# One load in place of two at the start of a decode block, and the two result stores in another written order

## The chip, the cores and the metric

The kernel runs on one core of a Trainium2 chip. The metric is the device time of one execution in microseconds (us); before the change it is 213.88 us, the median of three runs (213.80, 213.88 and 213.93 us).

## What is computed

The reference is one decode step of a transformer block for four sequences (B = 4, one token each, width D = 448), all in float32:

```python
h  = x + attention(layernorm(x))            # 16 query heads, 8 key/value heads of 256
h2 = h + mlp(layernorm(layernorm(h)))       # 448 -> 1792 -> gelu -> 448, with biases
# attention: q = x @ wq; scores over the last W = 1024 cached positions, softmax, values, @ wo
# mlp:       gelu(y @ w1 + b1) @ w2 + b2
```

Keys, values and weights are used once each, so nearly every byte that the kernel moves is read from HBM exactly once: 88.2 MB in all.

## The kernel before, in words

The work is tiled by the eight key/value heads, called groups g = 0 to 7. For one group the kernel projects the normed x to queries (`project_q`, line 204), multiplies them with the keys (`scores`, line 224), takes the softmax, transposes the probabilities (`transpose_p`, line 250), multiplies with the values (`values`, line 262), and adds the group's part of the output projection (`heads`, `project_o`). After the last group come the residual, two layer norms folded into one row of steps, the MLP with `w1` and `w2`, and the stores.

The host packs keys, values, query weights and output weights into eleven arrays, `stream0` to `stream10`, in the order in which they are wanted (the table `LOADS`, line 41: each row is one array and lists its parts). Each array is 128 rows, one for each SBUF partition, of 39,936 to 57,344 bytes, and is loaded by one DMA into one slot of a ring of three SBUF slots (`ring`, line 75). The function `part` (line 92) is asked for a piece; where it isn't there yet, it takes the next array, a slot, and issues the load:

```python
            if src is streams_first:
                nc.sync.dma_start(t[:, : WC + X0], first)
            at = WC + X0 if src is streams_first else 0
            nc.sync.dma_start(t[:, at : at + src.shape[-1]], src)
```

So the first slot is filled by two DMAs: `first` (the query weights of group 0, x transposed, b1 and b2; 7,312 bytes a row) and `stream0` (keys of group 0 and query weights of group 1; 39,936 bytes a row). The loads of `stream1` and `stream2` follow at once, since the ring has three slots. Every later load waits on SyncE's queue (SP) until the slot's last readers are done: `stream3` takes the slot of `first` and `stream0`, and its last reader on TensorE is the projection of group 1's queries (line 207); `stream4` takes the slot of `stream1`, whose last reader is the first half of group 0's values (line 269). After the streams, the same ring takes the values of group 7, the last output weights, `w1` and `w2` (lines 126 to 131 and 373 to 389).

What uses `first`: lines 315 to 326 take x out of it, form mean and variance with small matmuls (lines 186 and 187), a power on GpSimd (line 201), write the normed x to `yT` (lines 323 to 325) and project group 0's queries. Lines 329 to 347 spread the biases and x over partitions by four transposes on TensorE (lines 341 to 346). Constants that need no load (`sel`, `fold`, `foldn`, `back`, lines 142 to 172) are made on VectorE (DVE).

TensorE's order is the order in which the code is written (`manual_schedule` for PE); the order on the other engines is set by a scheduler from the written code. A DMA signals its end on one of eight completion semaphores, taken in turn; a DMA that gets a semaphore waits for the DMA that had it before.

The end: the result, in `res`, is stored by two DMAs of 8 rows each, one issued from ScalarE's queue (ACT), one from SP (lines 518 to 520).

Of the kernel before, what the change touches and what calls it, by code (L numbers as in the profile page):

```python
# [30 lines left out]
WC = 4 * D  # L31
QU = KV // 4
X0 = 2 * ND * B + 4
# [3 lines left out]
def parts(kind, g, quarters=range(4)):  # L37
    return [(kind, g, i) for i in quarters]


LOADS = [
    [("q", 0, 0), *parts("k", 0), ("q", 1, 0)],
    [*parts("k", 1), ("q", 2, 0), *parts("v", 0, (0, 1))],
    [*parts("v", 0, (2, 3)), ("o", 0, 0), *parts("k", 2)],
    [("q", 3, 0), *parts("v", 1), ("o", 1, 0), *parts("k", 3, (0,))],
    [*parts("k", 3, (1, 2, 3)), ("q", 4, 0), *parts("v", 2, (0, 1, 2))],
    [*parts("v", 2, (3,)), ("o", 2, 0), *parts("k", 4), ("q", 5, 0)],
    [*parts("v", 3), ("o", 3, 0), *parts("k", 5, (0, 1))],
    [*parts("k", 5, (2, 3)), ("q", 6, 0), *parts("v", 4)],
# [6 lines left out]
def width(part):  # L56
    kind, g, _ = part
    if kind in "kv":
        return QU
    return WC + (X0 if (kind, g) == ("q", 0) else 0)  # L60
# [8 lines left out]
SCALE = DH ** -0.5  # L69

@with_exitstack
def block_kernel(ctx: ExitStack, tc, first, streams, v7, wo67, w1, w2, w2_low, out):
    nc = tc.nc
    const = ctx.enter_context(tc.tile_pool(name="const", bufs=1))
    ring = ctx.enter_context(tc.tile_pool(name="ring", bufs=3))
# [10 lines left out]
    def slot(name):  # L86
        return ring.tile([P, SLOT], F32, tag="t", name=name)

    held = {}
    streams_first = streams[0]  # L90

    def part(kind, g, i=0):
        while (kind, g, i) not in held:
            src = streams.pop(0)
            t = slot("stream")
            wanted = LOADS[len(LOADS) - len(streams) - 1]
            if src is streams_first:
                nc.sync.dma_start(t[:, : WC + X0], first)  # L98
            at = WC + X0 if src is streams_first else 0
            nc.sync.dma_start(t[:, at : at + src.shape[-1]], src)  # L100
            at = 0
            for one in wanted:
                held[one] = t[:, at : at + width(one)]
                at += width(one)
        return held[kind, g, i]
# [10 lines left out]
    def load_k(g, h, c):  # L116
        return part("k", g, 2 * h + c).rearrange("p (b k) -> p b k", b=B)
# [5 lines left out]
    def load_v(g, c):  # L123
        return part("v", g, c).rearrange("p (c b d) -> p c b d", c=2, b=B)
# [176 lines left out]
    def project_o(g, wt):  # L301
        for i in range(4):
# [6 lines left out]
            for j in range(4):  # L309
# [3 lines left out]
                )  # L313

    t0 = part("q", 0)
    xT = t0[:, WC : WC + ND * B].rearrange("p (a b) -> p a b", a=ND)
    d = work.tile([P, ND, B], F32, tag="d", name="d_x")
# [42 lines left out]
    for g in range(HKV):  # L360
# [11 lines left out]
        else:  # L372
# [9 lines left out]
            at = 0  # L382
# [101 lines left out]
    for i in range(2):  # L484
        for j in range(4):
            if i <= j:
                at = PAD + C * j - P * (j - 1 + i) if j else PAD
# [27 lines left out]
                w = tw2[:, W2L + (c - 9) * C : W2L + (c - 8) * C]  # L515
                nc.tensor.matmul(py[3 * Q :], gT_low[:, c - 9, :], w, start=False, stop=False)  # L516
    nc.vector.tensor_copy(res[:, :C], py)  # L517
    for i, queue in ((1, nc.scalar), (0, nc.sync)):
        at = i * H + LIFT
        queue.dma_start(out[2 * B * i : 2 * B * (i + 1)], res[at : at + 2 * B])  # L520

# [68 lines left out]
```

## Time and profile before

| what | before |
|---|---|
| median of three runs | 213.88 us |
| the profiled execution, its own time | 213.79 us |
| its span in the trace, first to last instruction | 212.0 us |
| PE busy / DVE / ACT | 142.4 / 37.0 / 24.5 us |
| moved by DMA | 88.39 MB, mean 417 GB/s |
| SP's DMA queue (q1), share of the 16 DMA engines | 97.0% |
| chain that ended last | DMA 79%, PE 18% |

The span is 1.79 us shorter than the execution's own time; what lies outside is not in the trace. PE is the matmuls of TensorE, DVE VectorE, ACT ScalarE, POOL GpSimd, SP SyncE, which here only issues DMAs. "DMA share" is the mean share of the core's 16 DMA engines that is busy, and GB/s what they move. An idle engine costs nothing unless the end waits for it: what matters is which engine is never idle.

### The profile page before, as it was taken

To read this page: it belongs to the slowest core of one execution; us is meant where nothing else is said; L and a number is where in the kernel's file an instruction comes from. 1 tells how busy PE (TensorE), PEld (TensorE's weight loads), DVE (VectorE), ACT (ScalarE), POOL (GpSimd) and SP (SyncE) were. 2 spreads that over 40 slices of the span, in tenths; PEclk is the share of its full clock that TensorE was granted. 3 is DMA by queue.
4 is the path that set the end of the run, shared out by engine and by line. 5 is a ranking of instruction groups with operands and counts; after the bars stand their busy time and mean duration, and the time that the engine had idled before them with its cause. 6 is when DMAs were issued, how large, how long until landed. Compare 5 with 4: busy or idle time off the path is not lost.

```text
span 212.0 us, 2559 instructions
## 1 busy us (share of the span) xinstructions
PE 142.4 (67%) x1103; PEld 55.5 (26%) x1103; DVE 37.0 (17%) x153; ACT 24.5 (12%) x58; POOL 6.5 (3%) x22
## 2 busy tenths in 40 slices
PE   0469805861860885870794780586499998989994
PEld 0333301220110511220122120131124333335443
DVE  1521400320130110320123011031032032101330
ACT  2011300110001100210003000030002002100310
POOL 6200000000000000000000000000000000000110
PEclk9999975896697579996589698599589999999999
DMA  7999798999989999898999989899999899999991
GB/s 297 437 407 510 340 512 383 460 446 398 480 355 507 393 449 452 386 483 347 510 414 436 468 383 469 365 490 398 464 414 444 378 467 399 408 434 417 416 404 58
DMA packets 3146, 88.39 MB, mean 417 GB/s; under 512 B 368, under 2 KB 576, under 8 KB 960
## 3 DMA queue, kind: packets, MB, share of 16 engines
q1 hardware_dynamic: 3120, 88.24, 97.0%
q8 instruction: 8, 0.13, 0.2%
q14 instruction: 2, 0.02, 0.0%
q10 hardware_dynamic: 16, 0.00, 0.0%
HBM read 88.23 MB, written 0.01 MB: 416 GB/s over the span
## 4 chain that ended last, share of the span: by engine, by line
DMA 79%; PE 18%; ACT 1%; issue 0%; SPq 0%; DVE 0%; ACTq 0%
DMA stream<-stream 69%; DMA w<-w 10%; PE s L230 6%; PE po L269 6%; PE ppt L255 2%; PE py L510 2%; PE pq L207 1%; PE pqt L215 1%; ACT qs L209 1%; PE acc L304 0%; SPq L98 0%; SPq L100 0%; DVE res L517 0%; PE py L516 0%; ACTq L209 0%
## 5 line engine op out<-in xcount | busy, mean ns | idle before, releaser
L230 PE MATMUL s<-stream,qT 128*32 128x512 f32 x256 | 37.4, 730 | 17.1 <-DMA stream<-stream 17.1
L269 PE MATMUL po<-stream,pT 128*32 128x512 f32 x224 | 31.6, 702 | 17.5 <-DMA stream<-stream 17.5
L234 DVE TENSOR_REDUCE mx<-s 128x1 f32<-128x512 f32 x16 | 11.1, 691 | 57.3 <-PE s L230 57.3
L230 PEld LDWEIGHTS s<-stream,qT 128*32 128x32 f32 x256 | 9.7, 132 | 42.6 <-issue 30.6
L207 PE MATMUL pq<-stream,yT 128*32 128x512 f32 (+1 forms) x80 | 10.2, 603 | 9.7 <-DMA stream<-stream 6.6
L269 PEld LDWEIGHTS po<-stream,pT 128*32 128x32 f32 x224 | 6.9, 124 | 35.3 <-DMA stream<-stream 20.4
L286 DVE TENSOR_SCALAR o<-po,rec 128x256 f32<-128x256 f32 x8 | 3.9, 483 | 60.1 <-PE po L269 60.1
L209 ACT COPY qs<-pq 128x512 f32<-128x512 f32 x8 | 4.7, 585 | 83.3 <-PE pq L207 83.3
L287 ACT ACTIVATE o<-po,rec 128x256 f32<-128x256 f32 x8 | 3.8, 473 | 74.4 <-DVE o L286 74.4
L241 ACT ACTIVATE p<-s,nm 128x512 f32<-128x512 f32 x16 | 10.9, 689 | 10.1 <-DVE nm L237 10.1
L255 PE MATMUL ppt<-ident,p 128*128 128x128 f32 x64 | 11.1, 303 | 0.4
L304 PE MATMUL acc<-stream,oT 128*32 128x448 f32 x48 | 7.3, 683 | 5.2 <-DMA stream<-stream 4.0
L215 PE MATMUL pqt<-ident,qs 128*128 128x128 f32 x32 | 6.1, 322 | 5.7 <-ACT qs L209 5.7
L294 PE MATMUL pot<-ident,o 128*128 128x128 f32 x32 | 7.1, 317 | 3.8 <-DVE o L286 3.1
L354 PEld LDWEIGHTS <-idle 128*32 128x32 bf16 x70 | 6.3, 96 | 9.0 <-issue 3.6
L207 PEld LDWEIGHTS pq<-stream,yT 128*32 128x32 f32 x80 | 4.1, 124 | 17.1 <-issue 16.0
L255 PEld LDWEIGHTS ppt<-ident,p 128*128 128x128 f32 x64 | 7.6, 151 | 3.7 <-ACT p L241 3.7
L354 PE MATMUL tail<-idle 128*32 128x512 bf16 x28 | 7.6, 381 | 0.0
L294 PEld LDWEIGHTS pot<-ident,o 128*128 128x128 f32 x32 | 3.4, 148 | 13.3 <-DVE o L286 10.5
L354 PE MATMUL wait<-idle 128*32 128x512 bf16 x30 | 6.8, 380 | 0.0
L215 PEld LDWEIGHTS pqt<-ident,qs 128*128 128x128 f32 x32 | 3.9, 159 | 10.3 <-ACT qs L209 8.6
L462 POOL MEMSET u<- 128x64 f32 x1 | 0.2, 151 | 175.3 <-PE hsum L408 175.3
(128 smaller groups left out, 79.3 us busy)
## 6 DMA issues: line engine op xcount, KB each, us to landing
stream<-stream SPq DMA_DIRECT2D x5, 7040.0 KB, 35.8
stream<-stream SPq DMA_DIRECT2D x3, 6912.0 KB, 39.3
stream<-stream SPq DMA_DIRECT2D x2, 4992.0 KB, 16.1
stream<-stream SPq DMA_DIRECT2D x1, 7168.0 KB, 40.2
w<-w SPq DMA_DIRECT2D x2, 1792.0 KB, 21.4
v<-v SPq DMA_DIRECT2D x1, 3072.0 KB
w<-wo SPq DMA_DIRECT2D x1, 1792.0 KB, 19.6
w<-w SPq DMA_DIRECT2D x1, 1344.0 KB
```

What stands on the lines that cost most here:

```text
L207: nc.tensor.matmul(pq[j * Q : (j + 1) * Q, cols], yT[:, a, :], w, start=True, stop=True)
L209: nc.scalar.copy(qs, pq)
L215: nc.tensor.transpose(pt[:, i * P : (i + 1) * P], qs[:, i * P : (i + 1) * P], ident)
L230: nc.tensor.matmul(s[h][b * Q : (b + 1) * Q, :], qT[g % 2][:, c, b, :], load_k(g, h, c)[:, b, :], start=(c == 0), stop=(c == 1),)
L234: nc.vector.reduce_max(mx[:, h : h + 1], s[h], axis=AX.X)
L241: nc.scalar.activation(p[:, h * 512 : (h + 1) * 512], s[h], AF.Exp, bias=nm, scale=SCALE, accum_out=sums[:, h : h + 1],)
L255: nc.tensor.transpose(pt[:, c, :], p[:, c * P : (c + 1) * P], ident)
L269: nc.tensor.matmul(po[b * Q : (b + 1) * Q], pT[g % 2][:, c, b, :], vt[:, :, b, :], start=(c == 0), stop=(c == NKC // 2 - 1),)
L294: nc.tensor.transpose(pt[:, at : at + P], o[:, i, c * P : (c + 1) * P], ident)
L304: nc.tensor.matmul(acc[i * Q : (i + 1) * Q, :], oT[g % 2][:, i, :], wt[:, i, :], start=(g == 0), stop=(g == HKV - 3),)
L354: nc.tensor.matmul(to[:Q, :512], idle[:, :Q], idle, start=True, stop=True)
L510: nc.tensor.matmul(py[j * Q : (j + 1) * Q], beside(gT[:, c, :], j), w2t[c][:, j * C : (j + 1) * C], start=False, stop=(c == NFC - 1 or (c ...
```

## The change

The two loads of the first slot become one: the host joins the array `first` to the front of `stream0`, whose rows are now 47,248 bytes long (11,812 float32), and `part` has no special case for the first array. In the loop of the stores the pair that is issued from SP is now written ahead of the pair from ACT; each engine stores the same rows of `res` to the same place as before.

```diff
-def block_kernel(ctx: ExitStack, tc, first, streams, v7, wo67, w1, w2, w2_low, out):
+def block_kernel(ctx: ExitStack, tc, streams, v7, wo67, w1, w2, w2_low, out):
...
-            if src is streams_first:
-                nc.sync.dma_start(t[:, : WC + X0], first)
-            at = WC + X0 if src is streams_first else 0
-            nc.sync.dma_start(t[:, at : at + src.shape[-1]], src)
+            nc.sync.dma_start(t[:, : src.shape[-1]], src)
...
-    for i, queue in ((1, nc.scalar), (0, nc.sync)):
+    for i, queue in enumerate((nc.sync, nc.scalar)):
         at = i * H + LIFT
         queue.dma_start(out[2 * B * i : 2 * B * (i + 1)], res[at : at + 2 * B])
...
-    streams = {f"stream{i}": np.concatenate([part(*one) for one in load if one != ("q", 0, 0)], axis=1) for i, load in enumerate(LOADS)}
+    streams = {f"stream{i}": np.concatenate([part(*one) for one in load], axis=1) for i, load in enumerate(LOADS)}
```

Three places show what moves. The first is SP's queue at the start of the program, before the change (a name such as `stream_137` is an SBUF slot's tile, DMAHW0 to DMAHW7 are the eight completion semaphores):

```order
L98 DMA stream_137<-first 128x1828
L100 DMA stream_137<-stream0 128x9984
L100 DMA stream_254<-stream1 128x14080
L100 DMA stream_321<-stream2 128x14080
L100 DMA stream_375<-stream3 128x13824 [waits DMAHW0_49,DMAHW1_49,DVE_49,PE_49]
L100 DMA stream_442<-stream4 128x14080 [waits DMAHW2_49,PE_49]
```

The same place with the change:

```order
L96 DMA stream_137<-stream0 128x11812
L96 DMA stream_253<-stream1 128x14080
L96 DMA stream_320<-stream2 128x14080
L96 DMA stream_374<-stream3 128x13824 [waits DMAHW0_49,DVE_49,PE_49]
L96 DMA stream_441<-stream4 128x14080 [waits DMAHW1_49,PE_49]
```

One row is gone, every later DMA takes the semaphore one number lower, and the load of `stream3` waits for one DMA less in the same slot.

The second is the end of SP's queue, with the store on ACT's queue behind it, first before the change and then with it:

```order
L388 DMA w2_936<-w2_low 32x1x224 [waits DMAHW4_49]
L385 DMA w2_936<-w2 128x896 [waits DMAHW5_49]
L385 DMA w2_936<-w2 128x336 [waits DMAHW6_49]
L520 DMA out<-res_1094 8x128 [waits DMAHW0_49,DVE_49,Pool_49]
...
L520 DMA out<-res_1094 8x128 [waits DMAHW7_49,DVE_49,Pool_49]
```

```order
L384 DMA w2_935<-w2_low 32x1x224 [waits DMAHW3_49]
L381 DMA w2_935<-w2 128x896 [waits DMAHW4_49]
L381 DMA w2_935<-w2 128x336 [waits DMAHW5_49]
L516 DMA out<-res_1093 8x128 [waits DMAHW7_49,DVE_49,Pool_49]
...
L516 DMA out<-res_1093 8x128 [waits DMAHW6_49,DVE_49,Pool_49]
```

All numbers are one lower (0 becomes 7), so each DMA waits for the same earlier DMA as before: the two stores for the two pieces of `w1`, ACT's store for the first and SP's for the second. ACT's store has the earlier semaphore of the two in both kernels.

The third is VectorE at the start, from the last of its memsets to the normed x, before the change:

```order
L168 MEMSET idle 128x256
L331 COPY zT<-stream 128x16 [waits DMAHW0_49,DVE_49]
...
L189 TENSOR_REDUCE cm_sx<-pm_sx 128x4 [waits PE_49]
L200 TENSOR_SCALAR ve_x<-cm_sx 128x4 [waits DVE_49]
L143 TENSOR_TENSOR sel<-ident 128x32 [waits Pool_49]
...
L172 COPY back<-ident 128x4x4 [waits Pool_49]
L323 TENSOR_TENSOR yT<-d_x,rx 128x3x4 [waits Pool_49]
```

With the change:

```order
L164 MEMSET idle 128x256
L139 TENSOR_TENSOR sel<-ident 128x32 [waits Pool_49]
...
L168 COPY back<-ident 128x4x4 [waits Pool_49]
L327 COPY zT<-stream 128x16 [waits DMAHW0_49]
...
L185 TENSOR_REDUCE cm_sx<-pm_sx 128x4 [waits PE_49]
L196 TENSOR_SCALAR ve_x<-cm_sx 128x4 [waits DVE_49]
L319 TENSOR_TENSOR yT<-d_x,rx 128x3x4 [waits Pool_49]
```

The thirteen operations that make `sel`, `fold`, `foldn` and `back` have moved ahead of everything that waits for x.

## Rows read from the trace of the kernel before

**Rows 1.** The page: DMA share by 40 slices, and the chain that ended last.
```profile
DMA  7999798999989999898999989899999899999991
DMA 79%; PE 18%; ACT 1%; issue 0%; SPq 0%; DVE 0%; ACTq 0%
```

**Rows 2.** Busy time by stretches of the span, with its heading.
```profile
core 0: us, PE busy (x) PEld busy (x) DVE busy (x) ACT busy (x) POOL busy (x), PEclk, DMA share, GB/s
0.00:3.00 3.00, 0.00 (x0) 0.00 (x0) 0.85 (x6) 1.28 (x1) 2.43 (x13) 1.00 0.35 95
17.30:34.20 16.90, 8.80 (x54) 3.23 (x54) 3.03 (x12) 1.93 (x5) 0.00 (x0) 0.85 0.99 427
34.20:52.00 17.80, 10.73 (x70) 3.65 (x70) 2.78 (x11) 1.94 (x5) 0.00 (x0) 0.79 1.00 433
150.00:205.00 55.00, 51.47 (x423) 21.01 (x423) 10.10 (x38) 8.00 (x20) 1.51 (x4) 0.95 1.00 424
205.00:208.40 3.40, 3.13 (x97) 2.61 (x95) 0.69 (x4) 0.00 (x0) 0.00 (x0) 1.00 0.74 285
```

**Rows 3.** SP's timeline: start, us, what; the issues of `first`, `stream3` and `stream4`.
```profile
0.73 0.41 SPq L98 DMA_DIRECT2D stream<-first  x1
...
24.31 0.33 SPq L100 DMA_DIRECT2D stream<-stream  x1
...
45.92 0.33 SPq L100 DMA_DIRECT2D stream<-stream  x1
```

**Rows 4.** DMA view of windows 0:2.8, 2.8:4.3, 6:15, 18:30: packets, MB, share of 16 engines.
```profile
q1 hardware_dynamic: 31, 0.23, 32.3%
...
q1 hardware_dynamic: 83, 0.61, 96.1%
...
q1 hardware_dynamic: 100, 3.99, 102.5%
...
q1 hardware_dynamic: 96, 5.41, 104.1%
```

**Rows 5.** Timeline of the start: start us, us, engine, line, what [idle before <-releaser].
```profile
5.62 0.57 PE L186 MATMUL pm_x<-stream,mean 128*128 128x12 f32 x2 [5.62 <-DMA stream<-first]
...
9.00 1.03 POOL L201 TENSOR_TENSOR rx<-ve_x,mhalf 128x4 f32<-128x4 f32 x1 [4.95 <-DVE sel L143]
...
11.34 0.17 DVE L323 TENSOR_TENSOR yT<-d_x,rx 128x12 f32<-128x12 f32 x1
...
11.66 1.93 PE L207 MATMUL pq<-stream,yT 128*32 128x512 f32 x10 [3.15 <-DVE yT L324]
...
16.66 0.42 PE L346 MATMUL px<-ident,b1s 128*128 128x128 f32 x1
...
17.41 5.97 PE L230 MATMUL s<-stream,qT 128*32 128x512 f32 x32 [0.32 <-DMA stream<-stream]
...
23.19 1.05 PE L207 MATMUL pq<-stream,yT 128*32 128x512 f32 x10
...
25.69 1.32 PE L255 MATMUL ppt<-ident,p 128*128 128x128 f32 x8
```

**Rows 6.** TensorE's timeline: the second group's scores, and where PE waits for `stream2`.
```profile
34.31 6.05 PE L230 MATMUL s<-stream,qT 128*32 128x512 f32 x32 [7.30 <-DMA stream<-stream]
...
52.06 3.64 PE L269 MATMUL po<-stream,pT 128*32 128x512 f32 x16 [6.21 <-DMA stream<-stream]
...
58.32 3.62 PE L230 MATMUL s<-stream,qT 128*32 128x512 f32 x32
```

**Rows 7.** Timeline of the end: the last matmuls, the result's copy, the two stores.
```profile
205.78 2.14 PE L510 MATMUL py<-w,gT 128*32 128x112 f32 x74 [0.19 <-DMA w<-w]
...
209.40 0.27 DVE L517 COPY res<-py 128x112 f32<-128x112 f32 x1 [3.60 <-PE py L510]
...
209.74 0.32 SPq L520 DMA_DIRECT2D out<-res  x1
209.75 0.64 ACTq L520 DMA_DIRECT2D out<-res  x1
```

More of the change, by code (lines that the diff above doesn't have):

```diff
@@ L89, in block_kernel @@
     held = {}
-    streams_first = streams[0]
     def part(kind, g, i=0):
@@ L558, in part @@
             return (k if kind == "k" else v)[g][:, i * QU : (i + 1) * QU]
-        if kind == "q":
-            return wq[g]
-        return wo[g]
-    streams = {f"stream{i}": np.concatenate([part(*one) for one in load if one != ("q", 0, 0)], axis=1) for i, load in enumerate(LOADS)}
+        return first if (kind, g) == ("q", 0) else wo[g] if kind == "o" else wq[g]
+    streams = {f"stream{i}": np.concatenate([part(*one) for one in load], axis=1) for i, load in enumerate(LOADS)}
     w1 = packed(np.asarray(B_w1))
@@ L573 @@
     arrays = {
-        "first": first, **streams, "v7": v[-1], "wo67": np.concatenate([wo[-2], wo[-1]], axis=1), "w1": w1, "w2": w2, "w2_low": w2_low,
+        **streams, "v7": v[-1], "wo67": np.concatenate([wo[-2], wo[-1]], axis=1), "w1": w1, "w2": w2, "w2_low": w2_low,
     }
@@ L585 @@
             n = len(LOADS)
-            block_kernel(tc, args[0], args[1 : 1 + n], *args[1 + n :], out)
+            block_kernel(tc, args[:n], *args[n:], out)
     r = run(nc, [arrays], core_ids=[0])
```

## The prediction

> **What bounds the kernel now.** I read the page first: the DMA engines are busy in every slice but the first and the last, and the chain that ended last is DMA for 79% of the span [rows 1]. That chain alone doesn't say which transfers count, so I read the stretches next. From 17.3 us on, the DMA share is 0.99 to 1.00 at 424 to 433 GB/s, and stays there to 205 us [rows 2]. Sixteen engines that are never idle for 188 us are the bound: the kernel ends when its bytes are in, plus a start in which they are not yet busy (share 0.35 in the first 3 us [rows 2]) and an end after the last rows. TensorE waits for transfers in between (7.30 us at 34.31, 6.21 us at 52.06 [rows 6]) and at the end once more, for a piece of the last weights, at 205.78 [rows 7]. So an edit counts if it changes the bytes or the rows that the DMA engines work through, if it lets them run dry, or if it lengthens the 6.2 us from 205.78 to the end of the span at 212.0.
>
> **The transfer that goes.** `first` is 128 rows of 7,312 bytes, `stream0` 128 rows of 39,936; now it is 128 rows of 47,248. The bytes are the same. The price of a row comes from the DMA view: a stretch's share, times 16 engines, times its length, over its packets [rows 4]. A share over 100% means that a packet is counted where it starts.
>
> - 7,312 bytes: 0.961 × 16 × 1.5 us / 83 = 0.278 us.
> - 39,936 bytes: 1.025 × 16 × 9 us / 100 = 1.476 us, which is 27.06 kB per us.
> - 56,320 bytes: 1.041 × 16 × 12 us / 96 = 2.08 us, the same rate.
>
> At that rate 47,248 bytes take 1.746 us, against 0.278 + 1.476 = 1.754 us for the two rows of before: 0.008 us saved for each row, and with 128 rows over 16 engines 8 × 0.008 = **0.06 us** per engine. The bounds from these rows are 0 (the 0.008 us belongs to the layout of the rows and comes back) and 0.06; I take 0.06, since the two long rows agree with one rate to 0.1%.
>
> What could hide in that 0.008 us is a rule of the Trainium skill that speaks against this change, in "DMA: Bandwidth & Descriptors", section "How a descriptor splits into AXI transactions": a piece of memory that doesn't start at a multiple of 256 bytes costs extra beats. Rows of 39,936 bytes keep to such multiples and rows of 47,248 bytes don't. By the rule, one extra transaction in 185 would be an estimated 0.01 us a row and cancel the gain: the sum would be 0 instead of −0.06 us. The rows of `first` don't keep to multiples either, and their whole excess over the rate is 0.008 us, so the trace allows the rule no more than that.
>
> **The start-up.** In the first 2.8 us 31 rows took 0.323 × 16 × 2.8 us / 31 = 0.467 us each instead of 0.278 [rows 4]: an excess of 31 × 0.189 / 16 = 0.37 us per engine. What becomes of it with long rows no row shows. From below: it goes altogether, −0.37 us. From above: each engine's first row is slowed by the same factor of 1.68, so 0.68 × 1.746 = 1.19 us, that is 0.8 us more than now. The nearest row is the next stretch, 2.8 to 4.3 us, where rows of the same transfer already go at full rate: the slowness ends at a point in time and not after some share of a row. I take **0**.
>
> **What the later arrival of x does.** The first matmul could start at 5.62 us, when `first` was in; now x comes with the keys, at about 17.4 us, where TensorE had `stream0` before [rows 5]. Everything between moves behind that. Before, it took from 5.62 to 17.08 (the last of the four spreading transposes, 16.66 + 0.42): 11.46 us. Of this VectorE's constants go: GpSimd's power ended at 10.03 (9.00 + 1.03), but the normed x was written only at 11.34, behind `sel`, `fold`, `foldn` and `back`; these now run while the load is under way. That takes 1.3 us off, so the first scores start at about 17.4 + 10.2 = 27.6 us, and not at 17.41.
>
> Who waits for this? The scores and the projection of group 1 took 24.24 − 17.41 = 6.83 us [rows 5], so the first slot is free at about 34.4 us, and SP issues `stream3` then, 10.1 us later than the 24.31 of before [rows 3]. But at that time the queue still holds `stream2`, for which TensorE waits until 52.06 [rows 6]. An issue needs some 1.2 us until the engines are full (issue at 0.73 [rows 3]; idle for 0.65 × 3 = 1.95 us of the first three [rows 2]), and an engine may be a row of 2.1 us ahead of the last, so `stream3` has to be issued by about 48.7 us. **14 us of slack are left, cost 0.**
>
> The delay shrinks at the second group already. The transposes of the probabilities end 27.01 − 17.41 = 9.6 us after the first scores begin, at 37.2 us; the second scores then start there and not at 34.31, 2.9 us late. They may run at the shorter of the two times that these 32 matmuls show, 3.62 instead of 6.05 us [rows 6], because TensorE no longer stands idle ahead of them (mean granted clock 0.79 in the stretch from 34.2 [rows 2], between its two levels). So they end between 40.8 and 43.3 us, against 40.36, and `stream4`, issued at 45.92 before, goes out between 46.4 and 48.8. That has until `stream3` is in, some 16 us after `stream2`. The 6.21 us of idle time that TensorE has ahead of 52.06 take up the rest: from there I expect the old times.
>
> **The stores.** The rows of order for SP and ACT show the same two stores, at the same places in their queues, waiting for the same two earlier loads and for the same copy; both went out within 0.01 us of each other [rows 7]. Cost 0: this half of the change does nothing.
>
> **The sum.** −0.06 + 0 + 0 + 0 = −0.06 us on the profiled execution's 213.79 us (span 212.0 and 1.79 outside it): 213.73. The median of the runs stands 0.09 us above that execution, so 213.82, and I predict **213.8 us**. About 0.2%, or 0.43 us, is what a measurement of this kernel can tell from no change. The engines don't end together: in the last 3.4 us their share is 0.74 [rows 2], so the mean engine has stopped 0.26 × 3.4 = 0.9 us before 208.4, and which one is last may change a little. I allow half of that, 0.44 us, either way. With the start-up's lower bound the range is **213.4 to 214.3**.
>
> **Rivals.**
>
> *Each transfer has a price of its own.* If the engines stood idle for the 1.2 us of an issue between two transfers, one transfer less would give 213.88 − 1.2 = 212.7 us. For it speaks only that `first` is small. Against it: all the issues at the start go out early, so the next rows are always there, and the stretches with transfers' ends in them show 0.99 and 1.00 [rows 2]. Chance 0.04.
> The Trainium skill has a rule that points this way: the same page, section "Anatomy of one DMA — SWDGE (gpsimd) path", fits each DMA as some 2.0 us fixed plus its bytes. Summed over transfers, that would be 211.9 us as an estimate; in this kernel they overlap, and the trace's 1.00 leaves no room for it.
>
> *The ring runs dry (slower).* Place: the wait of SP ahead of `stream3`. Mechanism: the first slot is freed by work that now begins 11.8 us later. It decides from 48.7 us on, and from there each us of delay is a us of the end. If the 17.0 us from landing to release took twice as long, the issue would come at 51.4, and the time would be 213.9 + 2.7 = 216.6 us. For it: TensorE at the start is on SP's path. Against it: every piece of that work has a row, and 14 us are missing. Chance 0.02.
>
> *The slow first rows grow with the row.* 213.88 + 0.8 = 214.7 us. Chance 0.03.
>
> **Chances.** The forecast, within 0.43 us, has 0.86. Faster: 0.04 for the price of a transfer, and 0.03 for a start-up excess that goes while the engines' ends also fall well, together 0.07. Slower: 0.03 + 0.02, and 0.02 for the engines' ends falling badly, 0.07.
>
> **What would show it.** Right: one load in the first slot, TensorE's first matmul at about 17.4 us, the first scores at 27 to 28, `stream3` issued at 34 to 35, the wait for `stream2` ending at 52 as before, a DMA share of 1.00 from 17.3 on, PE's last wait for a weight within 0.4 us of 205.78. Wrong: a stretch with a share under 0.97 around 50 to 55 us (ring dry); the first matmul later than 18 us (start-up); every landing from the second on 1 us earlier (a transfer's own price); a later gap between the last matmul and the end of the span than the 2.6 us from 209.40 to 212.0 (stores).

## The result, and the profile after

The changed kernel takes 214.22 us (median of 14 runs, 213.93 to 214.43), the kernel before 213.78 us (median of 14 runs, 213.66 to 213.93). The ratio is 1.0019, with a 95% interval of 1.0012 to 1.0027: the change makes the kernel 0.44 us slower. That is a small loss, but clear of the noise; it lies inside the range that was given, and no change had been forecast.

The head of the page and its DMA rows, after; they answer to [rows 1]:

```profile
span 212.4 us, 2555 instructions
DMA  8999897999989899998999999899999899999991
q1 hardware_dynamic: 2976, 88.24, 97.0%
DMA 70%; PE 25%; ACT 1%; issue 1%; DVE 1%; POOL 0%; ACTq 0%
```

The span is 0.4 us longer, 212.4 us. The bytes are the same, 88.24 MB on SP's queue, in 144 packets fewer. The queue still fills 97.0% of the span, so its engines are busy for some 0.4 us more (0.970 × 212.4 = 206.0 us against 0.970 × 212.0 = 205.6 us), though they have fewer rows to go through. That is the first thing to explain.

The DMA view of the windows 0 to 2.8 us and 5.2 to 15 us, after (packets, MB, share of 16 engines); they answer to [rows 4]:

```profile
q1 hardware_dynamic: 16, 0.76, 94.3%
...
q1 hardware_dynamic: 89, 4.21, 99.1%
```

A row of 47,248 bytes takes 0.991 × 16 × 9.8 us / 89 = 1.746 us once the load is under way. But the first row of each engine, sixteen of them, takes 0.943 × 16 × 2.8 us / 16 = 2.64 us: 0.89 us too much on each engine. Before, the excess in the same window was 0.37 us.

TensorE's timeline of the start, after; it answers to [rows 5] and [rows 6]:

```profile
17.73 0.57 PE L182 MATMUL pm_x<-stream,mean 128*128 128x12 f32 x2 [17.73 <-DMA stream<-stream]
...
22.50 1.93 PE L203 MATMUL pq<-stream,yT 128*32 128x512 f32 x10 [1.88 <-DVE yT L320]
...
27.93 5.25 PE L226 MATMUL s<-stream,qT 128*32 128x512 f32 x32
...
36.76 3.64 PE L226 MATMUL s<-stream,qT 128*32 128x512 f32 x32
...
51.77 3.56 PE L265 MATMUL po<-stream,pT 128*32 128x512 f32 x16 [5.87 <-DMA stream<-stream]
```

The first slot is in at 17.73 us, and was at 17.41: 0.32 us later. The work that begins with x comes 10 to 12 us later than before, and all of that delay is gone at 51.77, where TensorE waits 5.87 us for `stream2`, as it did before.

SP's timeline, the issues of `stream3` and `stream4`, after [rows 3]:

```profile
34.12 0.33 SPq L96 DMA_DIRECT2D stream<-stream  x1
...
45.96 0.33 SPq L96 DMA_DIRECT2D stream<-stream  x1
```

`stream3` goes out 9.8 us later than before, `stream4` at the same time.

The timeline of the end, after [rows 7]:

```profile
206.08 2.14 PE L506 MATMUL py<-w,gT 128*32 128x112 f32 x74 [0.19 <-DMA w<-w]
...
209.69 0.27 DVE L513 COPY res<-py 128x112 f32<-128x112 f32 x1 [3.59 <-PE py L506]
210.03 0.32 SPq L516 DMA_DIRECT2D out<-res  x1
210.04 0.64 ACTq L516 DMA_DIRECT2D out<-res  x1
```

Every row stands 0.29 or 0.30 us later, and from one to the next nothing has changed: the last weights land later, and the end follows. So the loss is there when the first slot lands, 0.32 us, and is there when the last weights land, 0.30 us. In between, single landings don't show it (`stream2` came 0.29 us earlier, 51.77 against 52.06). But a landing is that of the slowest of the sixteen engines. The trace has sixteen completions for every load, and their mean shows the loss all the way: 17.10 us against 16.83 for the first slot, 50.53 against 50.28 for `stream2`, 204.77 against 204.52 for the last weights that TensorE waits for. Two profiles alone still don't prove that the long rows at the start are the cause. The runs do.

### The profile page after: what moved, and what is told of

It is laid out like the page before. It is cut to its first block, busy times and chain, and to the rows that moved or that the text cites. A ratio compares the mean times of both kernels' runs of the same rounds, so it can differ in the third digit from the quotient of the medians.

```text
span 212.4 us, 2555 instructions
## 1 busy us (share of the span) xinstructions
PE 140.1 (66%) x1103; PEld 54.9 (26%) x1103; DVE 39.1 (18%) x153; ACT 24.5 (12%) x58; POOL 6.5 (3%) x22
## 3 DMA queue, kind: packets, MB, share of 16 engines
q1 hardware_dynamic: 2976, 88.24, 97.0%
## 4 chain that ended last, share of the span: by engine, by line
DMA 70%; PE 25%; ACT 1%; issue 1%; DVE 1%; POOL 0%; ACTq 0%
DMA stream<-stream 60%; DMA w<-w 10%; PE s L226 8%; PE po L265 6%; PE pq L203 3%; PE ppt L251 2%; PE pqt L211 2%; PE py L506 2%; ACT qs L205 1%; POOL rx L197 0%; PE acc L300 0%; PE pb L337 0%; PE pm_sx L182 0%; PE pm_x L182 0%; PE pm_sx L183 0%
## 5 line engine op out<-in xcount | busy, mean ns | idle before, releaser
L226 PE MATMUL s<-stream,qT 128*32 128x512 f32 x256 | 36.2, 709 | 12.0 <-DMA stream<-stream 12.0
L265 PE MATMUL po<-stream,pT 128*32 128x512 f32 x224 | 29.5, 663 | 15.1 <-DMA stream<-stream 15.1
L226 PEld LDWEIGHTS s<-stream,qT 128*32 128x32 f32 x256 | 9.2, 128 | 36.3 <-issue 22.1
L203 PE MATMUL pq<-stream,yT 128*32 128x512 f32 (+1 forms) x80 | 11.0, 650 | 8.5 <-DMA stream<-stream 6.6
L182 PE MATMUL pm_x<-stream,mean 128*128 128x12 f32 x2 | 0.6, 362 | 17.7 <-DMA stream<-stream 17.7
```

The costliest lines, as they stand in the source:

```text
L203: nc.tensor.matmul(pq[j * Q : (j + 1) * Q, cols], yT[:, a, :], w, start=True, stop=True)
L226: nc.tensor.matmul(s[h][b * Q : (b + 1) * Q, :], qT[g % 2][:, c, b, :], load_k(g, h, c)[:, b, :], start=(c == 0), stop=(c == 1),)
L265: nc.tensor.matmul(po[b * Q : (b + 1) * Q], pT[g % 2][:, c, b, :], vt[:, :, b, :], start=(c == 0), stop=(c == NKC // 2 - 1),)
```

## Experiments

Two theories stood against each other. The **start-up theory**: long rows at the start of the load are slow, and what the engines lose there they never get back, since they have no idle time afterwards. The **late-x theory**: the loss comes from TensorE's work at another time. Two smaller ones were a price of the joined array (the number of loads, or where its rows begin) and a price of the issues of the next loads. Each time below is a median, with the ratio to the kernel before on the same chip and its 95% interval. "Landing" is the time at which TensorE, waiting for nothing else, took up the first slot's last piece, from one profile of each kernel.

**Late x, short rows first (q1_first).**

```diff
-    [("q", 0, 0), *parts("k", 0), ("q", 1, 0)],
+    [("q", 1, 0), ("q", 0, 0), *parts("k", 0)],
...
-            nc.sync.dma_start(t[:, : src.shape[-1]], src)
+            n = src.shape[-1]
+            cuts = [0, WC, n] if wanted is LOADS[0] else [0, n]
+            for a, b in zip(cuts, cuts[1:]):
+                nc.sync.dma_start(t[:, a:b], src[:, a:b])
```

> First slot in two loads again, but the first is the query weights of group 1 (7,168 bytes a row) and the second is x, the biases, group 0's query weights and the keys: x is as late as in the changed kernel, the program's first rows are as short as before. Start-up theory (the first row on each DMA engine is slowed, and a long one more): the 0.44 us go, 213.8 us, and the rows that start in the first 2.8 us have an excess of some 0.4 us per engine, as before. Late-x theory (the cost is TensorE's work at another time): 214.2 us.

Measured: 213.79 us, ratio 1.0003 (0.9994 to 1.0012). TensorE's first matmul:

```profile
17.34 0.57 PE L185 MATMUL pm_x<-stream,mean 128*128 128x12 f32 x2 [17.34 <-DMA stream<-stream]
```

x is nearly as late as in the changed kernel (17.34 us against 17.73), and the time is that of before. So late x costs nothing that can be told from zero, and the late-x theory falls. The stores are in the changed order in this kernel too, and cost nothing either.

**Long rows first, two loads (k0_first).** The same edit with the row `[*parts("k", 0), ("q", 1, 0), ("q", 0, 0)]` and the cut at `KV + WC`.

> First slot in two loads, keys and group 1's query weights first (39,936 bytes a row), then x with group 0's query weights (7,312 bytes). The number of loads is that of before, the first rows are long and x is late. Start-up theory: excess of some 0.8 us per engine, 214.2 us. A price of the joined array or of the number of loads: 213.8 us.

Measured: 214.25 us, ratio 1.0024 (1.0013 to 1.0034); landing at 18.04 us. The number of loads is that of before and the time is that of the changed kernel. The windows 0 to 2.8 us and 2.8 to 3.2 us:

```profile
q1 hardware_dynamic: 15, 0.60, 78.6%
...
q1 hardware_dynamic: 1, 0.04, 23.2%
```

The first rows of fifteen engines take 0.786 × 16 × 2.8 us / 15 = 2.35 us, instead of 1.476 [rows 4]. The sixteenth engine begins after 2.8 us, and its first row takes 0.232 × 16 × 0.4 us = 1.48 us, the full rate.

**The joined array, cut as before (cut_7k).** The loop of cuts with `cuts = [0, WC + X0, n]`, and the parts in the changed kernel's order.

> The joined array of the changed kernel (47,248 bytes from row to row), loaded in two column pieces of 7,312 and 39,936 bytes, as before. Start-up theory and late-x theory: 213.8 us, as before. If the layout of the joined array (rows that start at no multiple of 256 bytes) is what costs: 214.2 us.

Measured: 213.85 us, ratio 1.0003 (0.9994 to 1.0012); landing at 17.38 us. The layout in HBM costs nothing that can be told from zero, and the cut gives the 0.4 us back. (x is early again as well, but by q1_first that is worth nothing.) The window 0 to 2.8 us:

```profile
q1 hardware_dynamic: 24, 0.18, 37.7%
```

Here 24 rows take 0.704 us each instead of 0.278, an excess of 24 × 0.426 / 16 = 0.64 us per engine, and the slot still lands as early as before. By the same reckoning q1_first, ramp, standstill and cut_3k, which begin with short rows too, have 0.55 to 0.65 us, so the 0.37 us of the kernel before is the lowest of its kind. The mean excess in this window is a rough measure: it leaves out the time for which an engine that begins late stands idle. What the end follows is the landing, which is the slowest engine's (table below).

**Rows that begin at multiples of 256 bytes (pitch).**

```diff
-            nc.sync.dma_start(t[:, : src.shape[-1]], src)
+            n = sum(map(width, wanted))
+            nc.sync.dma_start(t[:, :n], src[:, :n])
...
+    streams["stream0"] = np.pad(streams["stream0"], ((0, 0), (0, 28)))
```

> The changed kernel with the joined array's rows 47,360 bytes apart in HBM (28 unused numbers behind each), so that every row starts at a multiple of 256 bytes; the load is the same. If the start of the rows costs: 213.8 us. If the length of the first rows costs: 214.2 us, and the rows after the first take 1.746 us each in both.

Measured: 214.24 us, ratio 1.0020 (1.0011 to 1.0029); landing at 17.77 us. The DMA view of 8 to 15 us has the same row in this kernel as in the changed one:

```profile
q1 hardware_dynamic: 65, 3.07, 101.3%
```

That is 1.013 × 16 × 7 us / 65 = 1.746 us a row in both. The rule of the Trainium skill on pieces that don't begin at multiples of 256 bytes ("DMA: Bandwidth & Descriptors", section "How a descriptor splits into AXI transactions") can't be seen at rows of this length.

**The next loads held back (hold_12).**

```diff
-            t = slot("stream")
+            t = early.pop(0) if early else slot("stream")
...
+    early.extend(slot("stream") for _ in range(3))
+    for t in early[1:]:
+        nc.gpsimd.memset(t[:, :1], 0.0)
```

> The changed kernel, with the loads of stream1 and stream2 held back until GpSimd has cleared a column of their slots, at about 4 us; the queue has 17 us of the first load to go through then. If the slow first rows come from the issue of the next loads beside them: excess back to 0.4 us or less, 213.8 us or below. If they are slow by themselves: 0.9 us, 214.2 us.

Measured: 214.22 us, ratio 1.0020 (1.0012 to 1.0029); landing at 17.88 us. The first sixteen rows are slow though no other load is issued before 4.12 us (0.889 × 16 × 2.8 us / 16 = 2.49 us). SP's two issues, and the window 0 to 2.8 us:

```profile
4.12 0.82 SPq L97 DMA_DIRECT2D stream<-stream  x2
...
q1 hardware_dynamic: 16, 0.76, 88.9%
```

**How the price goes with the length (cut_23k, cut_12k, cut_3k).** The loop of cuts with `[0, 5906, n]`, `[0, 3000, n]` and `[0, 914, WC + X0, n]`.

> The joined array loaded in two column pieces of 23,624 bytes a row each; x comes with the first. Rows of 7.2 kB at the start gave 213.8 us, rows of 39.9 and 47.2 kB 214.2 us. If the price grows with the length of the first row: between them, 213.9 to 214.1 us, and stream0's keys land 0.1 to 0.25 us later than in the kernel before. If only a short row escapes: 214.2 us. If it is the number of loads: 213.8 us.

> The joined array cut into 12,000 and 35,248 bytes a row. Rows of 7.3 kB gave 213.8 us and rows of 23.6 kB 214.1 us: if the price grows with the length of the first row, 213.8 to 214.0 us.

> The kernel before with its short first load cut once more: 3,656, 3,656 and 39,936 bytes a row. If the slowness is gone after a row, shorter rows save some 0.1 us: 213.7 us. If it is gone after a time, or 7.3 kB are short enough: 213.8 us, as before.

Measured: 214.12 us for 23.6 kB rows (1.0017, 1.0008 to 1.0025), 214.01 us for 12.0 kB (1.0010, 1.0001 to 1.0019), and 214.00 us for twice 3.7 kB (1.0009, 1.0000 to 1.0018). Against the kernel before on the same chip that is 0.1 us for 7.3 kB (cut_7k, within what can be told from none), 0.2 for 12.0 kB, 0.3 for 23.6 kB and 0.44 to 0.49 us for 39.9 and 47.2 kB: the price grows with the length of the first row, and not in proportion. The kernels with first rows of 7.3, 12.0, 23.6 and 39.9 kB (cut_7k, cut_12k, cut_23k, k0_first) all fill the slot with two loads, so that the number of loads doesn't make this order. The step from 7.3 to 12.0 kB isn't sure, since two kernels with short first rows but three loads in the slot, cut_3k and ramp (below), stand at 0.2 us as well. Neither time expected of cut_3k came: shorter rows than 7.3 kB gain nothing, and why the kernel is slower than with 7.3 kB stays open.

**Only x in front (tiny_first).** The first load is 36 columns, x and the biases, laid at the front of the array; the cut is at `X0`.

> x and the biases alone come first, 144 bytes a row, and the rest of the joined array (47,104 bytes a row) behind them. If the slowness belongs to the first row that an engine takes, the tiny rows take it up: 213.8 us or a little below. If it belongs to the first microsecond of the load, the long rows meet it: 214.2 us as in the changed kernel.

Measured: 214.51 us, ratio 1.0035 (1.0023 to 1.0048), the worst of these and above both times expected. The long rows begin only in the window from 2.21 to 2.7 us, since their issue comes behind the small one's:

```profile
q1 hardware_dynamic: 16, 0.75, 552.2%
```

And they are slow all the same: 5.522 × 16 × 0.49 us / 16 = 2.71 us for 47,104 bytes, 0.97 us over the rate. So the slowness isn't that of the first row that an engine takes, since tiny rows went ahead. Nor does it end at 2.8 us, from where the rows of the kernel before were at full rate [rows 4]: a row that begins at 2.21 us at the earliest and loses 0.97 us is slow until 3.1 us at least. The later beginning of the long rows, half a microsecond, comes on top.

**Both loads at once (two_queues).** The cuts of cut_7k, with the short load issued by `nc.scalar`.

> The loads of the kernel before, but the short first one is issued from ScalarE's queue and the long one from SP, at the same time. If short rows at the start help only by keeping long rows away from it: the long rows start at 1.7 us too and are slow, 214.1 us or more. If what helps is that each engine has a short row to begin with, or that the engines are filled sooner by two queues: 213.8 us or less.

Measured: 214.30 us, ratio 1.0022 (1.0012 to 1.0033); landing at 18.19 us. The window 0 to 2.8 us:

```profile
q1 hardware_dynamic: 15, 0.60, 76.0%
```

The first fifteen rows in this kernel are long ones, at 0.760 × 16 × 2.8 us / 15 = 2.27 us instead of 1.476. Short rows help only where the long ones come behind them.

**Short rows for twice as long (ramp).** Cuts at `WC + X0` and `WC + X0 + QU`: 7,312, 8,192 and 31,744 bytes.

> The joined array cut into 7,312, 8,192 and 31,744 bytes a row: short rows for twice as long. If the engines were at full rate already when the long rows of the kernel before began: 213.8 us, the same as before. If short rows still help later: below 213.7 us.

Measured: 214.03 us, ratio 1.0012 (1.0003 to 1.0020). There is no gain, which fits engines that are at full rate after the first short load. But neither of the expected times came, and the 0.2 us of loss, which cut_3k shows too, isn't explained by these runs.

**A second start in the middle (standstill).**

```diff
-            t = slot("stream")
+            t = early.pop(0) if early else slot("stream")
...
     t0 = part("q", 0)
+    early.extend([slot("stream"), slot("stream")])
+    for t in early:
+        nc.gpsimd.tensor_copy(t[:, :1], part("k", 0, 3)[:, :1])
```

with the cuts of cut_7k.

> Loads of 7,312 and 39,936 bytes a row as before, but stream1 and stream2 are issued only when the keys have landed (GpSimd copies a key into a column of each of their slots first), so that all DMA engines stop at about 17 us and start again together with rows of 56,320 bytes. If the engines are slow only at the start of a program: the first row of each takes 2.08 us as everywhere else, and the stop costs its own 2 us, some 215.7 us. If long rows are slow whenever all engines start from a standstill: these 16 rows take 2.7 to 3.1 us, and the time is some 216.3 us.

Measured: 216.81 us (two runs), ratio 1.0141 (1.0122 to 1.0159), 0.5 us above the higher of the two times expected. SP's issue, the DMA view of 18 to 19.5 us, of 18.4 to 18.65 us, of 19.2 to 19.5 us and of 20 to 30 us, and TensorE's wait for `stream1`:

```profile
17.49 0.33 SPq L100 DMA_DIRECT2D stream<-stream  x1
...
q1 hardware_dynamic: 16, 0.90, 179.6%
...
q1 hardware_dynamic: 9, 0.51, 657.0%
...
q1 hardware_dynamic: 2, 0.11, 86.5%
...
q1 hardware_dynamic: 78, 4.39, 101.5%
...
37.42 5.09 PE L230 MATMUL s<-stream,qT 128*32 128x512 f32 x32 [11.54 <-DMA stream<-stream]
```

The sixteen rows after the stop take 1.796 × 16 × 1.5 us / 16 = 2.69 us each, the rows from 20 us on 1.015 × 16 × 10 us / 78 = 2.08 us. Nine of the sixteen begin within a quarter of a microsecond and take 6.570 × 16 × 0.25 us / 9 = 2.92 us; the two that begin last take 0.865 × 16 × 0.3 us / 2 = 2.08 us, the full rate. So the start of the program is nothing special: long rows are slow at a start from a standstill, in the first microseconds and at 18 us alike. It is the rows that show this and not the time: of the 3.0 us lost, 0.6 us are slow rows, and the rest comes with the stop (the keys land at 17.4 us, and no row of `stream1` begins before 18.4). `stream1` is 3.11 us later than before (37.42 against 34.31), and the whole kernel 3.0 us: here too, what the engines lose once is lost at the end.

The kernels by their landing of the first slot, where TensorE waits for it and the profile so shows it. "Last weights" is the end of TensorE's wait for the last weights in the same profile, 205.78 us in [rows 7]; the median is that of all runs.

| kernel | first rows, bytes | landing, us | last weights, us | median, us |
|---|---|---|---|---|
| q1_first | 7,168 | 17.34 | 205.65 | 213.79 |
| cut_7k | 7,312 | 17.38 | 205.76 | 213.85 |
| before | 7,312 | 17.41 | 205.78 | 213.78 |
| cut_3k | 3,656 | 17.60 | 205.99 | 214.00 |
| changed | 47,248 | 17.73 | 206.08 | 214.22 |
| pitch | 47,248 | 17.77 | 206.11 | 214.24 |
| hold_12 | 47,248 | 17.88 | 206.24 | 214.22 |
| k0_first | 39,936 | 18.04 | 206.43 | 214.25 |
| two_queues | 39,936 beside 7,312 | 18.19 | 206.40 | 214.30 |
| tiny_first | 144, then 47,104 | 18.42 | 206.40 | 214.51 |

Within one execution the landing is handed on to the end: in eight of the ten kernels the last weights come 188.3 to 188.4 us after it, whether it is early or late, and whatever TensorE does in between. In the two with the latest landings some of the loss is made up on the way (188.21 and 187.98 us). The median rises with the landing too, though less at the long end, where one profile's landing is a single draw. No version is faster than the kernel before.

## Why the prediction was wrong

**The step that failed** is the start-up, "I take 0"; it is a term of the sum that was given the wrong size. In its place the runs showed that long rows from a standstill cost time: the first slot lands 0.32 us later (17.73 us against 17.41) although the rows saved give back 0.06 us, so that the term is some +0.4 us, and the table shows that the landing is handed on to the end. By the rows of the first window the excess is 0.89 instead of 0.37 us per engine, 0.52 us more, which with the 0.06 us of the rows saved would make 0.46 us, against 0.44 measured. That this comes so close is luck: with the 0.64 us of cut_7k, which has the time of the kernel before, the same sum gives 0.89 − 0.64 − 0.06 = 0.19 us.

The bounds of the term, −0.37 to +0.8 us, held; the value between them was chosen for a wrong reason. The nearest row was taken to be the next stretch, with short rows at full rate, and from that it was read that the slowness ends at a point in time. tiny_first and standstill show that it doesn't: long rows that start together are slow from 2.2 us and from 18.4 us on too. The next stretch was the wrong neighbour, since its rows are short ones that follow others on engines already under way. The only rows of that trace that had started from a standstill were those of the first 2.8 us, and they couldn't decide between a loss of fixed size and one that grows with the row.

The range took in the lower of these bounds and left out the upper. That 214.22 us lies in it is owed to the 0.44 us that were allowed for another cause, the engines' ends. The sign that was named for the start-up, a first matmul later than 18 us, didn't come (17.73), since it had been set for the upper bound. And the kernel before took 213.78 us this time, 0.10 us less than in the three runs that the forecast started from, so the change was missed by 0.50 us (−0.06 forecast, +0.44 measured).

The rival *the slow first rows grow with the row* came nearest, with a chance of 0.03 that was far too small: longer first rows do cost more. Its rule, the factor of 1.68 whatever the length, doesn't hold: the long row's factor was 2.64 / 1.746 = 1.51, and in standstill, with 56,320 bytes, 2.69 / 2.08 = 1.29. The loss of an engine is 0.6 to 1.0 us with long rows and 0.37 to 0.65 us with short ones.

**What held.** The row's price: 1.746 us forecast, 1.746 measured. The later x: first scores at 27.93 us (27.6 forecast), `stream3` issued at 34.12 (34.4), second scores at 36.76 and at the short one of their two times, 3.64 us (37.2 and 3.62), everything caught up before `stream2` lands; and q1_first shows that the cost can't be told from 0, as said. The first matmul came at 17.73 instead of 17.4, which is the start-up again. The stores: the same rows at the same distances from each other [rows 7], cost 0, which q1_first and cut_7k bear out, since they have the new order too.

**The other rivals.** A price of each transfer, with a gain of 1.2 us: no, k0_first and the changed kernel, with one load between them, differ by 0.03 us. The Trainium skill's 2.0 us fixed for each DMA ("DMA: Bandwidth & Descriptors", section "Anatomy of one DMA — SWDGE (gpsimd) path") are a fit to DMAs issued from GpSimd. Added up over these loads, which are issued from SP and queue behind each other, they can't be seen in these 0.03 us. The ring that runs dry: no, `stream3` went out at 34.12 us, 14 us ahead of the 48.7 us by which it was needed.

## What to carry to other kernels

In this kernel the DMA engines never idle, and what they lose at the start is paid at the end, whatever else hides behind the transfers. Here it paid to begin the load from a standstill with one transfer of short rows (7 kB, 0.3 us each at full rate) and to queue the long rows behind it: joining the two because fewer transfers look cheaper cost 0.44 us. Two short transfers (cut_3k, ramp) or one of tiny rows (tiny_first) did worse than the one. And where a cost has a bound on either side, look for rows that were in the same state, here engines that had just started, and not for the rows that came next; where those rows can't decide, both bounds belong in the range.

## What the runs showed that was not expected

A long row (39.9 to 56.3 kB) from a standstill takes 2.3 to 2.7 us in the mean where 1.5 to 2.1 us are usual: 0.6 to 1.0 us more, at the start of the program (changed kernel, hold_12, pitch, k0_first, two_queues), behind tiny rows (tiny_first), and in the middle (standstill). Where rows of 7 kB go first, alone, their own excess is 0.37 to 0.64 us, the slot lands 0.3 to 0.8 us earlier than with long rows first, and the long rows that follow run at full rate (1.476 us [rows 4]).

Why is open: the runs exclude the issue of other loads, the rows' beginnings in HBM, the number of loads and the first microseconds of the program, but don't show what the sixteen engines wait for when they start together. One finding narrows it: an engine that begins its long row late, when the others are under way, had the full rate at once in k0_first (1.48 us) and standstill (2.08 us). It is no rule, though: in hold_12 the engine that began last, at 2.79 us, took 2.39 us instead of 1.746.
